# Merging and single-buffering four small tiles, so that the tiles behind them lie 128 bytes lower

## The chip, the cores and the metric

The kernel runs on one core of a Trainium2 chip. The metric is the device time of one execution in microseconds. The kernel before takes 742.22 us (median of three runs, 741.92 to 744.39).

## What is computed

Windowed attention with a linear bias, and a gated feed-forward layer on its output, all in float32:

```python
scores = scale * q @ k.T - slope[h] * dist       # 4 batches, 8 heads, 768 tokens, head size 64
scores = where(keep, scores, -1e9)               # first n_global keys, and the last n_local before a token
a = exp(scores - max); a = a / (sum(a) + 1e-9)
x = (a @ v) as [3072 tokens, 512]
out = (sigmoid(x @ w_gate) * (x @ w_val)) @ w_out   # inner size 1536
```

With the inputs that are timed, n_global is 8 and n_local is 96, so that a tile of 128 queries needs at most 256 keys.

## The kernel before

Tokens are worked off in eight blocks of 384 (`blocks`, half a batch each). While the feed-forward part of one block runs, the attention of the next block is woven into it. The feed-forward part of a block has twelve rounds, one for each 128 of the 1536 inner columns. In a round, `ff_in` does two groups of twelve matmuls (L564): the stationary operand is a 128x128 piece of `w1l` or `w1h` (gate and value weights, split into a high and a low part), the moving one 384 columns of `xh` or `xl` (the attention output, split in the same way). They end in the PSUM tiles `ps_g` and `ps_u`, from which ScalarE and VectorE make `work`, `hh` and `hl`. `ff_out` then does nine matmuls (L604): a 128x128 piece of `hh` or `hl` stands, 512 columns of `w2l` or `w2h` (output weights) move; only the first six rounds of the first block work with unsplit `hh` and `w2f`. Woven in between stand the score matmuls of a query tile (L387, four of 256 columns: `qs` stands, `ks` moves) and the matmuls with V (L502). The order on each engine is made when the kernel is built, by a list scheduler that works with a model of the instructions' times.

SBUF is given out by pools that lie one behind the other. Ahead of the pool `small` lie `wpool` (`w1h`, `w1l`, `w2f`), `cpool` and `xpool` (`xh`, `xl`). `small` holds tiles of a few bytes in each partition, and each of its buffers takes 32 bytes. Behind it lie `mpool` (`work`, `hl`, `hh`), `w2pool` (`w2h`, `w2l`), `rpool` (`kr`, the K columns), `spool` (`v0`, `v1`, `pT`), and behind those `wraw` (raw weights, while they are converted) and later `late` (`qr`, `qs`, `ks`, `halves`, `turned`, `pT2`, `ost`). What `small` takes therefore shifts everything behind it. In a `ks` tile, the key slots of successive query tiles lie 640 bytes apart, which is 128 more than 512.

At the end stands a general path, for values of n_local and n_global that the windowed scheme can't serve. Its test runs always: `top` is the largest of the row minima `nms` (L752), it is turned by TensorE (L754), reduced to one number (L756), and compared, with n_local and n_global, against bounds (L764); the five answers in `fl` give one flag (L766), and each engine branches on it. With the timed inputs the path itself (`dense_block`, with `gnm`, `gsm` and `grc`) is jumped over, and only a memset of `fl` (L844) runs in its place.

Of the kernel before, what the change touches and what calls it, by code (L numbers as in the profile page):

```python
# [8 lines left out]
F32 = mybir.dt.float32  # L9
# [10 lines left out]
P = 128  # L20
# [8 lines left out]
def attn_moe_kernel(ctx, tc, qT, kT, v, n_global, n_local, wg, wv, wo, out, B, H, S, D):  # L29
# [18 lines left out]
    small = ctx.enter_context(tc.tile_pool(name="small", bufs=4))  # L48
# [699 lines left out]
    general = ctx.enter_context(ExitStack())  # L748
    gpool = general.enter_context(tc.tile_pool(name="gpool", bufs=1))
    late["pool"] = gpool  # L750
    top = small.tile([P, 1], F32, name="top", bufs=1)
    nc.vector.tensor_reduce(top, nms, axis=AX.X, op=ALU.max)  # L752
    ps = ps_a.tile([P, 4, P], F32, name="ps_t")
    nc.tensor.transpose(ps[0:1, 0], top, ident)  # L754
    fl = small.tile([1, 5], F32, name="fl", bufs=1)
    nc.vector.tensor_reduce(fl[:, 4:5], ps[0:1, 0], axis=AX.X, op=ALU.max)  # L756
    for i, (src, bound, op) in enumerate((
        (nf[0:1, 0:1], 1.0, ALU.is_lt),
# [9 lines left out]
    def dense_tables(t):  # L768
        reli = gpool.tile([P, S], I32, name="reli")
        nc.gpsimd.iota(reli, pattern=[[-1, S]], base=t * P, channel_multiplier=1)  # L770
        rel = gpool.tile([P, S], F32, name="rel")
        nc.vector.tensor_copy(rel, reli)
        keep = gpool.tile([P, S], F32, name="keep")
        pen = gpool.tile([P, S], F32, name="pen")
        dist = gpool.tile([P, S], F32, name="dist")
        nc.vector.tensor_scalar(keep, rel, nf[:, 0:1], None, op0=ALU.is_lt)
        nc.vector.tensor_scalar(pen, rel, 0.0, None, op0=ALU.is_ge)
        nc.vector.tensor_tensor(keep, keep, pen, op=ALU.mult)
        nc.gpsimd.iota(reli, pattern=[[1, S]], base=0, channel_multiplier=0)
        glo = gpool.tile([P, S], F32, name="glo")  # L780
        nc.vector.tensor_copy(glo, reli)
        nc.vector.tensor_scalar(glo, glo, nf[:, 1:2], None, op0=ALU.is_lt)
        nc.vector.tensor_tensor(pen, glo, keep, op=ALU.mult)
        nc.vector.tensor_tensor(glo, glo, pen, op=ALU.subtract)

        nc.vector.tensor_tensor(dist, rel, keep, op=ALU.mult)
        nc.vector.tensor_scalar(pen, glo, nf[:, 0:1], None, op0=ALU.mult)
        nc.vector.tensor_tensor(dist, dist, pen, op=ALU.add)
        nc.vector.tensor_tensor(keep, keep, glo, op=ALU.add)
        nc.vector.tensor_scalar(pen, keep, 1.0, 1.0e9, op0=ALU.subtract, op1=ALU.mult)  # L790
        return keep, pen, dist

    def dense_block(b, t0, xh, xl):
        for t in range(TB):
            keep, pen, dist = dense_tables(t0 + t)
            for s in range(NPAIR):
                r0 = b * (H * D) + 2 * s * D
                qg = gpool.tile([P, P], F32, name="qg")
                nc.sync.dma_start(qg, qT[bass.ds(r0, P), (t0 + t) * P:(t0 + t + 1) * P])
                kg = gpool.tile([P, S], F32, name="kg")  # L800
                nc.sync.dma_start(kg, kT[bass.ds(r0, P), :])
                vg = gpool.tile([P, NTB, P], F32, name="vg")
                nc.sync.dma_start(
                    vg, v[bass.ds(b * S, S), s * P:(s + 1) * P].rearrange("(t p) x -> p t x", p=P)
                )
                nc.vector.tensor_scalar(qg, qg, SCALE, None, op0=ALU.mult)
                av = ps_a.tile([P, 4 * P], F32, name="ps_v")
                for j in range(2):
                    hd = slice(j * D, (j + 1) * D)
                    sb = gpool.tile([P, S], F32, name="sb")  # L810
                    for c in range(S // NB):
                        cols = slice(c * NB, (c + 1) * NB)
                        ps = ps_gv.tile([P, NB], F32, name=("ps_g", "ps_u")[c % 2])
                        nc.tensor.matmul(ps, qg[hd], kg[hd, cols], start=True, stop=True)
                        nc.vector.scalar_tensor_tensor(
                            sb[:, cols], dist[:, cols], -slopes[2 * s + j], ps, op0=ALU.mult, op1=ALU.add
                        )
                    nc.vector.tensor_tensor(sb, sb, keep, op=ALU.mult)
                    nc.vector.tensor_tensor(sb, sb, pen, op=ALU.add)
                    nm = small.tile([P, 1], F32, name="gnm", bufs=2)  # L820
                    nc.vector.tensor_reduce(nm, sb, axis=AX.X, op=ALU.max, negate=True)
                    sm = small.tile([P, 1], F32, name="gsm", bufs=2)
                    nc.scalar.activation(sb, sb, AF.Exp, bias=nm, accum_out=sm)
                    nc.vector.tensor_scalar(sm, sm, 1e-9, None, op0=ALU.add)
                    rc = small.tile([P, 1], F32, name="grc", bufs=2)
                    nc.vector.reciprocal(rc, sm)
                    nc.vector.tensor_scalar(sb, sb, rc, None, op0=ALU.mult)
                    pT = gpool.tile([P, NTB, P], F32, name="gpT")
                    for c0 in range(0, NTB, 3):
                        pt = ps_a.tile([P, 4, P], F32, name="ps_t")  # L830
                        for c in range(3):
                            nc.tensor.transpose(pt[:, c], sb[:, (c0 + c) * P:(c0 + c + 1) * P], ident)
                        nc.scalar.copy(pT[:, c0:c0 + 3], pt[:, 0:3])
                    for c in range(NTB):
                        nc.tensor.matmul(
                            av[hd, 0:P], vg[:, c, hd], pT[:, c], start=(c == 0), stop=(c == NTB - 1)
                        )
                cols = slice(t * P, (t + 1) * P)
                nc.scalar.activation(xh[:, s, cols], av[:, 0:P], AF.Copy)
                nc.vector.tensor_tensor(xl[:, s, cols], av[:, 0:P], xh[:, s, cols], op=ALU.subtract)  # L840
# [4 lines left out]
    with fits.Else():  # L845
        with tc.For_i(0, B, 1) as b:
            for t0 in range(0, NTB, TB):
                blocks.append((b, t0, TB))
                bi = len(blocks) - 1
                xslot[bi] = (0, NC * NB)  # L850
                dense_block(b, t0, *x_of(bi))
                for f in range(NF):
                    split_w2(f)
                    ff_in(bi, f)
                    ff_out(bi, f)
# [39 lines left out]
```

## Time and profile before

| | us |
|---|---|
| median of three runs | 742.22 |
| the profiled execution, its own time | 743.09 |
| its span, first to last instruction | 741.2 |
| TensorE busy with matmuls | 725.1 |
| VectorE busy | 499.8 |
| ScalarE busy | 420.3 |
| GpSimd busy | 218.8 |

The profiled execution lies 0.87 us above the median, and 1.9 us of its time lie outside its span. The end of a matmul is modelled in the trace, and a matmul begins before the one ahead of it has ended; so the pace of a row of matmuls is read from the distance between their starts, not from their durations.

### The profile page before, as it was taken

The numbers are of one execution on the slowest core, as the hardware profiler recorded it, in microseconds if no ns is written. First come the engines' busy times: TensorE is split into PE (matmuls) and PEld (weight loads), VectorE is DVE, ScalarE is ACT, GpSimd is POOL, SyncE is SP. The second block draws the span as 40 slices with busy tenths as digits, with TensorE's granted clock in tenths as the row PEclk, the third lists the DMA queues.
The fourth block names the chain that finished last, engine by engine and source line by source line (L and its number), as shares of the span: only waits on it lengthen the run. The fifth ranks groups of instructions, "written<-read, shape, count | busy, mean of one in ns | idle before, by whom it ended". The sixth has DMA issues, their size and how long they took to land. (4 is left out here: it accounts for less than half of the span.)

```text
span 741.2 us, 12477 instructions
## 1 busy us (share of the span) xinstructions
PE 725.1 (98%) x4403; PEld 657.2 (89%) x4403; DVE 499.8 (67%) x1303; ACT 420.3 (57%) x948; POOL 218.8 (30%) x166
## 2 busy tenths in 40 slices
PE   7999999999999999999999999999999999999997
PEld 6667778989889999999999999999999999999996
DVE  7889799667877777676677868666786876321111
ACT  5797887756565565566456655655555664332222
POOL 6424355323231323223132322313233231221222
PEclk9999999999999999999999999999999999999999
DMA  8967662624537343432435442343335224010001
GB/s 253 279 193 243 188 193 75 159 62 88 104 78 159 84 105 70 99 103 63 83 80 117 112 105 63 62 123 73 95 80 109 71 46 83 15 44 1 1 0 46
DMA packets 136866, 74.27 MB, mean 100 GB/s; under 512 B 87136, under 2 KB 129120, under 8 KB 136800
## 3 DMA queue, kind: packets, MB, share of 16 engines
q1 hardware_dynamic: 136800, 73.43, 40.1%
q8 instruction: 36, 0.59, 0.3%
q14 instruction: 30, 0.25, 0.1%
HBM read 49.81 MB, written 6.29 MB: 76 GB/s over the span
## 5 line engine op out<-in xcount | busy, mean ns | idle before, releaser
L180 POOL TENSOR_TENSOR w2l<-w2f,w2h 128x512 fp32r<-128x512 f32 x89 | 121.3, 1363 | 377.5 <-ACT w2h L217 363.7
L581 DVE SCALAR_TENSOR_TENSOR work<-work,ps_u 128x384 f32<-128x384 f32 x90 | 49.7, 552 | 131.0 <-PE ps_u L564 126.8
L564 PE MATMUL ps_g<-xh,w1l 128*128 128x384 f32 x384 | 131.9, 343 | 1.0 <-ACT work L572 1.0
L564 PE MATMUL ps_u<-xh,w1l 128*128 128x384 f32 x384 | 131.5, 342 | 0.1
L564 PE MATMUL ps_g<-xl,w1h 128*128 128x384 f32 x384 | 130.7, 340 | 0.7 <-DVE xl L545 0.7
L564 PE MATMUL ps_g<-xh,w1h 128*128 128x384 f32 x384 | 130.4, 340 | 0.0
L564 PE MATMUL ps_u<-xh,w1h 128*128 128x384 f32 x384 | 130.0, 339 | 0.0
L564 PE MATMUL ps_u<-xl,w1h 128*128 128x384 f32 x384 | 129.9, 338 | 0.0
L584 ACT ACTIVATE hh<-work 128x384 fp32r<-128x384 f32 x90 | 46.9, 522 | 132.4 <-DVE work L581 132.2
L419 ACT ACTIVATE work<-work,nms 128x256 f32<-128x256 f32 (+1 forms) x192 | 92.0, 480 | 27.5 <-DVE nms L406 27.1
L604 PE MATMUL ps_o<-w2l,hh 128*128 128x512 f32 x267 | 105.0, 393 | 0.4 <-POOL w2l L180 0.4
L604 PE MATMUL ps_o<-w2h,hh 128*128 128x512 f32 x267 | 105.1, 394 | 0.0
L604 PE MATMUL ps_o<-w2h,hl 128*128 128x512 f32 x267 | 104.5, 394 | 0.0
L180 DVE TENSOR_TENSOR hl<-work,hh 128x384 fp32r<-128x384 f32 x90 | 79.5, 884 | 23.5 <-ACT hh L584 23.3
L217 ACT ACTIVATE w2h<-w2f 128x512 fp32r<-128x512 f32 x89 | 56.0, 629 | 54.2 <-PE ps_o L604 52.6
L564 PEld LDWEIGHTS ps_g<-xh,w1l 128*128 128x128 f32 x384 | 72.7, 189 | 5.2 <-issue 2.8
L564 PEld LDWEIGHTS ps_u<-xh,w1l 128*128 128x128 f32 x384 | 72.2, 188 | 4.0 <-issue 1.2
L564 PEld LDWEIGHTS ps_g<-xl,w1h 128*128 128x128 f32 x384 | 72.7, 189 | 2.7 <-DVE xl L545 1.1
L564 PEld LDWEIGHTS ps_u<-xl,w1h 128*128 128x128 f32 x384 | 72.3, 188 | 1.1
L564 PEld LDWEIGHTS ps_g<-xh,w1h 128*128 128x128 f32 x384 | 72.7, 189 | 0.5 <-issue 0.2
L438 DVE TENSOR_SCALAR work<-work,rc 128x256 f32<-128x256 f32 (+1 forms) x168 | 71.6, 465 | 2.0
L564 PEld LDWEIGHTS ps_u<-xh,w1h 128*128 128x128 f32 x384 | 72.2, 188 | 0.0
(133 smaller groups left out, 1171.8 us busy)
## 6 DMA issues: line engine op xcount, KB each, us to landing
qr<-in_qT SPq DMA_DIRECT2D x56, 192.0 KB, 3.4
kr<-in_kT SPq DMA_DIRECT2D x32, 192.0 KB, 2.6
v<-in_v SPq DMA_DIRECT2D x32, 192.0 KB, 3.7
raw<-in_w_gate SPq DMA_DIRECT2D x12, 512.0 KB, 4.2
raw<-in_w_val SPq DMA_DIRECT2D x12, 512.0 KB, 5.6
raw<-in_w_out SPq DMA_DIRECT2D x12, 512.0 KB, 3.7
out<-ost SPq DMA_DIRECT2D x24, 256.0 KB, 2.2
v<-in_v SPq DMA_DIRECT2D x16, 144.0 KB, 3.8
```

The costliest lines, as they stand in the source:

```text
L180: eng.tensor_tensor(out, a, b, op=ALU.subtract)
L217: ins = nc.scalar.activation(hi, w, AF.Copy)
L419: ins = nc.scalar.activation(sb[:, j, :w], sb[:, j, :w], AF.Exp, scale=-1.0, bias=nm[:, j:j + 1], accum_out=sm[:, j:j + 1])
L438: nc.vector.tensor_scalar(sb[:, j, :w], sb[:, j, :w], rc[:, j:j + 1], None, op0=ALU.mult)
L564: nc.tensor.matmul(ps[:, :n], wt[f][:, i, c], xt[:, c, :n], start=(k == 0), stop=(k == 3 * NC - 1))
L581: nc.vector.scalar_tensor_tensor(a[:, :n], a[:, :n], 1.0, pss[1][:, :n], op0=ALU.add, op1=ALU.mult)
L584: nc.scalar.activation(hh[:, :n], a[:, :n], AF.Copy)
L604: ins = nc.tensor.matmul(outs[bi][t], ht[:, t * P:(t + 1) * P], wt, start=(f == 0 and k == 0), stop=(f == NF - 1 and k == len(parts) - 1),)
```

## The change

The test's two tiles become columns of one: `top` is column 0 of a 128x6 tile, `fl` the columns 1 to 5 of its first partition. In the general path, `gnm`, `gsm` and `grc` have one buffer instead of two. That makes four buffers of 32 bytes less in `small`, and everything that lies behind `small` moves down by 128 bytes in each partition. No instruction that runs with the timed inputs is added, removed or given another shape.

```diff
-    top = small.tile([P, 1], F32, name="top", bufs=1)
+    last = small.tile([P, 6], F32, name="top", bufs=1)
+    top = last[:, 0:1]
     nc.vector.tensor_reduce(top, nms, axis=AX.X, op=ALU.max)
     ps = ps_a.tile([P, 4, P], F32, name="ps_t")
     nc.tensor.transpose(ps[0:1, 0], top, ident)
-    fl = small.tile([1, 5], F32, name="fl", bufs=1)
+    fl = last[0:1, 1:6]
...
-                    nm = small.tile([P, 1], F32, name="gnm", bufs=2)
+                    nm = small.tile([P, 1], F32, name="gnm", bufs=1)
...
-                    sm = small.tile([P, 1], F32, name="gsm", bufs=2)
+                    sm = small.tile([P, 1], F32, name="gsm", bufs=1)
...
-                    rc = small.tile([P, 1], F32, name="grc", bufs=2)
+                    rc = small.tile([P, 1], F32, name="grc", bufs=1)
```

## Rows read from the trace of the kernel before

**Rows 1.** The page's head and its first part: busy time of each engine, share, instructions.
```profile
span 741.2 us, 12477 instructions
PE 725.1 (98%) x4403; PEld 657.2 (89%) x4403; DVE 499.8 (67%) x1303; ACT 420.3 (57%) x948; POOL 218.8 (30%) x166
```
**Rows 2.** Table of stretches, TensorE: stretch, length, busy (matmuls), clock, DMA share, GB/s.
```profile
0.00:45.00 45.00, 38.16 (x305) 1.00 0.79 232
486.80:572.60 85.80, 85.80 (x526) 1.00 0.39 90
660.00:741.20 81.20, 75.76 (x395) 0.99 0.06 20
```
**Rows 3.** Groups of instructions, TensorE, 231 to 660 us: count, busy us, mean ns.
```profile
L564 PE MATMUL ps_g<-xl,w1h 128*128 128x384 f32 x240 | 80.9, 337 | 0.0
...
L564 PE MATMUL ps_u<-xh,w1h 128*128 128x384 f32 x237 | 80.3, 339 | 0.0
...
L604 PE MATMUL ps_o<-w2h,hh 128*128 128x512 f32 x180 | 70.9, 394 | 0.0
```
**Rows 4.** The same groups in two short stretches, 722.85 to 724.94 and 721.95 to 722.85.
```profile
L564 PE MATMUL ps_u<-xh,w1h 128*128 128x384 f32 x4 | 1.3, 336 | 0.0
...
L604 PE MATMUL ps_o<-w2h,hh 128*128 128x512 f32 x2 | 0.8, 389 | 0.0
```
**Rows 5.** The same groups in two others, 716.55 to 718.66 and 714.47 to 716.55.
```profile
L564 PE MATMUL ps_u<-xh,w1h 128*128 128x384 f32 x4 | 1.4, 340 | 0.0
...
L604 PE MATMUL ps_o<-w2h,hh 128*128 128x512 f32 x3 | 1.2, 395 | 0.0
```
**Rows 6.** Timeline of TensorE, 716 to 730 us: start us, us, instruction.
```profile
716.56 0.34 PE L564 MATMUL ps_u<-xh,w1l 128*128 128x384 f32 x1
...
718.51 0.34 PE L564 MATMUL ps_u<-xh,w1h 128*128 128x384 f32 x1
...
722.86 0.34 PE L564 MATMUL ps_u<-xh,w1l 128*128 128x384 f32 x1
...
724.77 0.34 PE L564 MATMUL ps_u<-xh,w1h 128*128 128x384 f32 x1
...
727.03 0.39 PE L604 MATMUL ps_o<-w2l,hh 128*128 128x512 f32 x1
...
729.11 0.34 PE L564 MATMUL ps_u<-xh,w1l 128*128 128x384 f32 x1
```
**Rows 7.** Table of stretches, all engines (PE, PEld, DVE, ACT, POOL busy), same stretch.
```profile
716.50:729.10 12.60, 12.60 (x67) 11.81 (x67) 2.23 (x4) 3.81 (x7) 3.37 (x3) 1.00 0.00 1
```
**Rows 8.** Timeline of TensorE, 318 to 326 us.
```profile
318.19 0.64 PE L387 MATMUL ps_s<-ks,qs 128*128 128x256 f32 x4
318.67 0.39 PE L604 MATMUL ps_o<-w2l,hh 128*128 128x512 f32 x1
...
320.70 0.34 PE L564 MATMUL ps_g<-xh,w1l 128*128 128x384 f32 x1
...
324.87 0.64 PE L387 MATMUL ps_s<-ks,qs 128*128 128x256 f32 x4
325.34 0.34 PE L564 MATMUL ps_g<-xh,w1l 128*128 128x384 f32 x1
```
**Rows 9.** Timeline of VectorE, 6 to 7 us and 658 to 659 us.
```profile
6.21 0.32 DVE L764 TENSOR_SCALAR fl<-nf 1x1 f32<-1x1 f32 x4
...
658.21 0.28 DVE L756 TENSOR_REDUCE fl<-ps_t 1x1 f32<-1x128 f32 x1 [0.42 <-PE ps_t L754]
```
**Rows 10.** Table of stretches, TensorE, around 60 us.
```profile
58.00:59.00 1.00, 0.00 (x0) 1.00 0.73 234
...
61.00:62.00 1.00, 1.00 (x5) 0.50 1.01 396
```
**Rows 11.** Timeline of TensorE, 60 to 64 us.
```profile
60.90 0.52 PE L564 MATMUL ps_g<-xh,w1l 128*128 128x384 f32 x1
...
63.46 0.47 PE L564 MATMUL ps_g<-xh,w1h 128*128 128x384 f32 x1
```

## The prediction

> **What bounds the kernel now.** I began with the busy times of the page: TensorE is busy with matmuls for 725.1 of 741.2 us, and no other engine for more than 499.8 [rows 1]. The table of stretches says where the remaining 16 us are: 6.8 in the first 45 us, where K, Q and the raw weights arrive, and 5.4 behind 660 us; in the stretch of a whole block there is no gap at all, 85.80 of 85.80 us [rows 2]. So in between, the time is the number of matmuls times their pace, and a change that adds and removes no instruction can only act through that pace, through the two ends, or through the order of the instructions.
>
> Therefore I read the pace next, from the starts of the matmuls in the timeline. It has two levels with the same operands. From 716.56 to 718.51 lie eleven distances between L564 matmuls, 1.95 us or 177 ns each; from 722.86 to 724.77 eleven more, 1.91 us or 174 ns each [rows 6]. For L604 the nine distances from 727.03 to 729.11 make 231 ns each [rows 6], and the nine from 318.67 to 320.70 make 226 ns [rows 8]. A round of 24 matmuls at L564 and nine at L604 is thus 0.09 + 0.05 us dearer at the slow pace (24 x 3.6 ns and 9 x 5.5 ns). The granted clock is 1.00, 2.4 GHz, through the stretch in which the pace switches [rows 7]. The mean durations follow the pace: 336 and 389 ns in fast stretches [rows 4], 340 and 395 in slow ones [rows 5]. Over 231 to 660 us the groups have 337 to 339 and 394 [rows 3]. For L604 that is (394 - 389) / (395 - 389), or 0.8 of the rounds at the slow pace. For L564 it is between 0.25 and 0.75, and rather too much, since a matmul behind a pause counts long too; I take 0.45.
>
> What sets the pace? Not other engines: in the stretch of rows 6, where it switches, VectorE is busy for 2.23, ScalarE for 3.81 and GpSimd for 3.37 of 12.6 us [rows 7], and the pace holds over whole groups. It is what went before. A round of L604 that follows directly on fast L564 matmuls is slow (727.03), and one that follows on a score group is fast (318.67) [rows 6, 8].
>
> The Trainium skill says in SBUF — State Buffer, section "Who interferes with whom", that TensorE and ScalarE never wait for another engine's access to SBUF. By that alone the place of a tile would be worth nothing and the time 742.2 us; by the rows the pace moves by 2 to 3% without another engine's help, which the rule neither foresees nor forbids, and the sum would lie anywhere between the bounds below. The trace agrees with the rule in that the switch doesn't follow the other engines.
>
> **The change, part by part.**
>
> The general path (three tiles with one buffer instead of two) doesn't run: what it would wait for costs 0. Its code may become some instructions longer or shorter, and the branch jumps over it. That lies behind the last L604 matmul; I take 0.
>
> The test: top and fl share a tile. The danger is order. Four of the five comparisons, L764, need only n_local and n_global, and the scheduler has put them at 6.21 us, 652 us ahead of L756 at 658.21, which in the program comes before them and writes the same tile fl, another column [rows 9]. So a tile's columns are followed one by one, and columns 1 to 4 of the shared tile can be written as early as before. Cost 0. If I am wrong, four instructions of together 0.32 us leave VectorE's queue in the first stretch and stand behind L756 at 658 us, where TensorE is far ahead in work. At most 0.3 us would be gained at the start, and nothing lost at 658 us. I count 0, and bound it by -0.3 and 0.
>
> The shift by 128 bytes. It touches the operands of L604 (hh, hl, w2h, w2l), L387 (ks, qs) and L502 (V, pT), and what VectorE, ScalarE, GpSimd and the DMAs read and write. It doesn't touch those of L564, for w1 and x lie ahead of the pool small. The trace has no move by 128 bytes of the same operand, but one near it: the key slots of successive score groups lie 128 bytes more than 512 apart. Four score matmuls take 318.67 - 318.19 = 0.48 us in one and 325.34 - 324.87 = 0.47 us in the next [rows 8], so a step of 128 bytes is worth at most 10 ns in 480, 2%, and the two groups are followed by different matmuls, which may be all of it. On the nine matmuls of L604 in 90 rounds (96 less the six unsplit ones) 2% would be 90 x 9 x 4.6 ns = 3.7 us either way; the direct cost I take is 0, because both operands of every shifted matmul move by the same amount and keep their distance.
>
> What remains is the hand-over, where a matmul with unshifted operands (L564) follows on one with shifted ones, or the reverse. If it depends on addresses, rounds change their pace. All of L604 and L564 fast would be 90 x 0.8 x 0.05 = 3.6 us and 96 x 0.45 x 0.09 = 3.9 us less, 7.5 in all; all slow 90 x 0.2 x 0.05 = 0.9 and 96 x 0.55 x 0.09 = 4.8 us more, 5.7 in all. Between -7.5 and +5.7 I take 0, by the row that is nearest, the two score groups, which differ by no more than the last digit.
>
> The first 45 us: transfers into shifted tiles. TensorE lacks 6.8 us there for all reasons together [rows 2], and nothing in the rows speaks for a transfer that is longer or shorter by its address; I take 0 and allow 0.5 either way.
>
> A shift of some tenths in the start can also move the half clock. After a time without a matmul at 58 to 59 us, TensorE is granted 0.50 of its clock, 1.2 instead of 2.4 GHz, at 61 to 62 us [rows 10], and from 60.90 to 63.46 eight matmuls come 320 ns apart [rows 11] instead of 174: 1.2 us that can go, or come a second time at another gap.
>
> Sum: 743.09 + 0 = 743.09 us against the profiled execution, which lay 0.87 above the median; so 742.2 us for a median.
>
> **The rivals.**
>
> *The fast hand-over.* The slow rounds of L604 are those behind fast L564 matmuls, the commonest sequence. If with the lower addresses this hand-over behaves as that behind a score group, L604 runs at 226 ns and the next L564 group starts fast. For it: most of L604 is on the slow side today (0.8), so there is more to win than to lose there. Against it: no row shows that an address decides it, and the time since the last pause could as well. Half of the 7.5 us gives 738.5 us. It passes 0.3% (2.2 us) when three rounds in ten turn.
>
> *The slow hand-over.* Slower than before: L564 is fast today in about half of its groups, those that follow on scores, V matmuls or a fast L604. If the last shifted operand ahead of them now leaves them at the slow pace, each round pays 0.09 us. Two thirds of the 4.8 us gives 745.4 us; it passes 0.3% when half of the fast groups turn. For it: L564 is the larger part of the matmuls. Against it: it needs the good hand-overs to go bad, all at different addresses.
>
> *The half clock goes or comes twice*: 741.0 or 743.4 us, within the forecast.
>
> *The comparisons move*: 741.9 us, within the forecast. That the change does nothing at all to the pace is the forecast itself.
>
> **How the numbers follow.** A measurement of this kernel tells about 0.3%, 2.2 us, from no change. No change that can be measured: 0.44, with a range of its own from 740.0 to 744.4. The fast hand-over: 0.33. The slow one: 0.23. The trace shows that the pace hangs on small things, which keeps the two rivals together above the forecast; it shows no address that decides it, which keeps each of them below it. The range of 8 in 10 reaches into both: down to 737.6, a little below the fast rival's time, and up to 745.8, a little above the slow one's.
>
> **What would show each step right or wrong.** Right: L604 with w2h and hh at a mean of 394 and L564 at 337 to 339 ns in the stretch from 231 to 660 us, a block of 85.8 us, L764 four times near 6.2 us. Fast hand-over: a mean of L604 near 389 to 391, with 226 ns between starts directly behind L564. Slow hand-over: L564 groups at 340 to 341. If the mean durations stay and the time moves, the step on the pace is wrong and the cause lies in the first 60 us, in the clock or in the order of instructions; if the number of matmuls between the stages differs, the step on the scheduler is wrong.

## The result and the profile after

The kernel after takes 736.58 us (median of seven runs, 735.94 to 741.15), the kernel before 743.28 in the runs made beside it (741.92 to 745.74). The ratio is 0.992, with a 95% interval from 0.989 to 0.995. That is faster by more than the 0.3% of the prediction, and 1.0 us under the low end of its range. The profiled execution took 736.18 us.

The page's head and its first part, of the kernel after, beside [rows 1]:

```profile
span 734.4 us, 12477 instructions
...
PE 718.1 (98%) x4403; PEld 653.0 (89%) x4403; DVE 498.8 (68%) x1303; ACT 420.2 (57%) x948; POOL 219.4 (30%) x166
```

Every engine ran as many instructions as before. The span fell by 6.8 us and TensorE's busy time by 7.0, while VectorE, ScalarE and GpSimd moved by 1.0 us at most. TensorE does the same matmuls in less time.

Table of stretches, TensorE, of after (stretch, length, busy and matmuls, granted clock, DMA share, GB/s). The second is the stretch around [rows 10, 11], the third holds the same 526 matmuls as the block of [rows 2], and the fourth the same 395 as its last stretch:

```profile
0.00:45.00 45.00, 37.57 (x303) 1.00 0.77 229
58.00:66.00 8.00, 7.27 (x54) 1.00 0.91 301
482.07:567.47 85.40, 85.40 (x526) 1.00 0.40 91
653.78:734.40 80.62, 75.05 (x395) 0.99 0.06 21
```

A block has no gap, as before, and takes 85.40 us instead of 85.80. The stretch from 58 to 66 us in the kernel before:

```profile
58.00:66.00 8.00, 6.61 (x44) 0.79 0.88 278
```

Groups of instructions on TensorE from 231 to 660 us in after, the lines of [rows 3] (count, busy us, mean ns):

```profile
L564 PE MATMUL ps_g<-xl,w1h 128*128 128x384 f32 x244 | 82.1, 336 | 0.0
...
L564 PE MATMUL ps_u<-xh,w1h 128*128 128x384 f32 x240 | 80.7, 336 | 0.0
L604 PE MATMUL ps_o<-w2h,hh 128*128 128x512 f32 x181 | 70.6, 390 | 0.0
```

L604 went from 394 to 390 ns and L564 from 337 and 339 to 336, which are, within 1 ns, the means of the fast stretches of [rows 4]. The timeline of TensorE in after shows a round of L604 directly behind L564 (start us, us, instruction):

```profile
707.60 0.34 PE L564 MATMUL ps_g<-xh,w1h 128*128 128x384 f32 x1
707.77 0.39 PE L604 MATMUL ps_o<-w2l,hh 128*128 128x512 f32 x1
...
709.81 0.34 PE L564 MATMUL ps_u<-xh,w1l 128*128 128x384 f32 x1
```

The nine distances from 707.77 to 709.81 make 227 ns each. In the kernel before, the same nine matmuls lie from 714.48 to 716.56, 231 ns each: the matmul at 709.81 is the one at 716.56 of [rows 6], and that at 707.77 is this one of before:

```profile
714.48 0.39 PE L604 MATMUL ps_o<-w2l,hh 128*128 128x512 f32 x1
```

**Where the 6.8 us came from.** Both kernels run the same 4403 matmuls in the same order, so the same matmul can be followed through both timelines. The one at 60.90 of [rows 11] starts at 59.99 in after, 0.9 us earlier; the one at 63.46 starts at 61.38, 2.1 earlier; the one at 716.56 starts at 709.81, 6.75 earlier. So 0.9 us came before 61 us, 1.2 from the half clock of [rows 10, 11], which this execution of after didn't have, and 4.7 from the pace of the matmuls in the 650 us behind it. The timelines of TensorE around 59 us show the first two, first before and then after (in brackets the idle time ahead and what ended it):

```profile
59.39 0.48 PE L373 MATMUL ps_v<-kr,qr 64*128 64x256 f32 x1 [1.84 <-DVE nms L406]
...
60.58 0.52 PE L564 MATMUL ps_g<-xh,w1h 128*128 128x384 f32 x1
60.90 0.52 PE L564 MATMUL ps_g<-xh,w1l 128*128 128x384 f32 x1
```

```profile
58.73 0.48 PE L373 MATMUL ps_v<-kr,qr 64*128 64x256 f32 x1 [0.84 <-DVE nms L406]
...
59.82 0.34 PE L564 MATMUL ps_g<-xh,w1h 128*128 128x384 f32 x1
59.99 0.34 PE L564 MATMUL ps_g<-xh,w1l 128*128 128x384 f32 x1
```

TensorE waited 1.84 us for VectorE's `nms` in the one and 0.84 in the other. Behind the long wait the matmuls come 320 ns apart, behind the short one 170. Neither is shown to come from the change. The wait differs from execution to execution: all_up128 below has the pace of before and a wait of 0.46 us. And a long wait doesn't always bring the half clock: TensorE waited 1.78 us in gnm_only, 1.85 in w2_up64 and 1.90 in kv_back, and was granted 1.00 from 58 to 66 us in all three. Here is gnm_only (wait, then stretch):

```profile
60.13 0.48 PE L373 MATMUL ps_v<-kr,qr 64*128 64x256 f32 x1 [1.78 <-DVE nms L406]
```

```profile
58.00:66.00 8.00, 6.22 (x51) 1.00 0.85 279
```

The 4.7 can be read from the starts in the timelines. From 100 us in the kernel before to the matmul at 716.56, the distances between the same matmuls add up to 4.5 us less in after: 2.2 us between two matmuls of L604, 1.8 between two of L564, and 0.5 in all other places. It can also be counted in groups. Behind 100 us I called an L564 group of twelve slow when its mean distance, the first distance left out, is above 175 ns, and an L604 round slow when it is above 230.3 ns. A slow L564 group costs 12 x 3.4 = 41 ns (176.8 instead of 173.4 ns a matmul), a slow round of L604 9 x 4.9 = 44 ns (231.6 instead of 226.7). A "decaying" round begins slow and becomes fast within its nine matmuls; where the line is drawn moves the counts of L604 by a few rounds.

```
                            before   after
L564 groups, slow / fast    70/105   6/169
L604 rounds, slow / decaying / fast   64/17/8   4/12/72
L604 directly behind fast L564        53 slow of 54   58 fast of 60
L564 directly behind L604             32 slow of 51   0 slow of 51
```

64 groups x 41 ns and 60 rounds x 44 ns are 2.6 + 2.6 = 5.2 us, an estimate that is 0.7 above the 4.5 read directly.

**What the median holds besides.** A half clock like that of [rows 10] comes in some executions and not in others, of either kernel. The 110 executions of the kernel before, in all comparisons below, have a median of 741.6 us where the mean granted clock of the execution was 0.998 or more (44 of them) and of 744.8 where it was 0.993 or less. The four executions of after at 0.998 have 736.2. At like clock the change is worth 5.4 us (0.7%), near the 4.7 of pace in the profiled pair and the 5.0 that up128 shows below. The remaining 1.3 of the 6.7 us between the medians I put down to how many half-clock stretches fell into these seven and seven runs; the granted clock of all seven runs of before is not on record, so this isn't shown.

### The profile page after: what moved, and what is told of

It reads as the page before. It is cut to its first block, busy times and chain, and to the rows that moved or that the text cites. A ratio compares the mean times of both kernels' runs of the same rounds, so it can differ in the third digit from the quotient of the medians.

```text
span 734.4 us, 12477 instructions
## 1 busy us (share of the span) xinstructions
PE 718.1 (98%) x4403; PEld 653.0 (89%) x4403; DVE 498.8 (68%) x1303; ACT 420.2 (57%) x948; POOL 219.4 (30%) x166
## 5 line engine op out<-in xcount | busy, mean ns | idle before, releaser
L564 PE MATMUL ps_g<-xh,w1l 128*128 128x384 f32 x384 | 131.1, 341 | 1.0 <-ACT work L572 1.0
L564 PE MATMUL ps_u<-xh,w1l 128*128 128x384 f32 x384 | 130.9, 341 | 0.1
L564 PE MATMUL ps_g<-xl,w1h 128*128 128x384 f32 x384 | 129.6, 337 | 0.7 <-DVE xl L545 0.7
L564 PE MATMUL ps_g<-xh,w1h 128*128 128x384 f32 x384 | 129.4, 337 | 0.0
L564 PE MATMUL ps_u<-xh,w1h 128*128 128x384 f32 x384 | 129.3, 337 | 0.0
L564 PE MATMUL ps_u<-xl,w1h 128*128 128x384 f32 x384 | 129.2, 336 | 0.0
L604 PE MATMUL ps_o<-w2l,hh 128*128 128x512 f32 x267 | 104.9, 393 | 0.6 <-POOL w2l L180 0.5
L604 PE MATMUL ps_o<-w2h,hh 128*128 128x512 f32 x267 | 104.1, 390 | 0.0
L604 PE MATMUL ps_o<-w2h,hl 128*128 128x512 f32 x267 | 103.1, 389 | 0.0
L564 PEld LDWEIGHTS ps_g<-xh,w1l 128*128 128x128 f32 x384 | 72.2, 188 | 5.1 <-issue 2.3
L564 PEld LDWEIGHTS ps_u<-xh,w1l 128*128 128x128 f32 x384 | 72.1, 188 | 3.9 <-issue 1.2
L564 PEld LDWEIGHTS ps_g<-xl,w1h 128*128 128x128 f32 x384 | 72.2, 188 | 2.6 <-DVE xl L545 1.1
L564 PEld LDWEIGHTS ps_u<-xl,w1h 128*128 128x128 f32 x384 | 72.2, 188 | 1.0
L564 PEld LDWEIGHTS ps_g<-xh,w1h 128*128 128x128 f32 x384 | 72.2, 188 | 0.5 <-issue 0.2
L564 PEld LDWEIGHTS ps_u<-xh,w1h 128*128 128x128 f32 x384 | 72.2, 188 | 0.0
```

The source lines that it names most:

```text
L564: nc.tensor.matmul(ps[:, :n], wt[f][:, i, c], xt[:, c, :n], start=(k == 0), stop=(k == 3 * NC - 1))
L604: ins = nc.tensor.matmul(outs[bi][t], ht[:, t * P:(t + 1) * P], wt, start=(f == 0 and k == 0), stop=(f == NF - 1 and k == len(parts) - 1),)
```

## The experiments

**The theory:** TensorE's pace hangs on where the operands of one stage lie against those of the other (w1 and x of L564 on one side, hh, hl and w2 of L604, K and V on the other). **The rivals:** the absolute address, so that lower is faster; the merged tile or the single buffers themselves, by order or by waits; and the distance of the two operands within a stage.

The last two columns are the counts from the timeline of each profiled execution; "at 0.998" is the median of the executions at that mean granted clock or more, with their number.

```
kernel       behind small lies   median us  ratio [95%]            at 0.998    L564 slow  L604 slow/decaying
before       as it is            743.3      1                      741.6 (44)  70         64/17
after        -128                736.58     0.992 [0.989, 0.995]   736.2 (4)    6          4/12
up128        +128                737.35     0.991 [0.989, 0.993]   736.5 (2)    6          3/14
up256        +256                742.97     1.000 [0.998, 1.002]   741.5 (4)   67         63/18
all_up128    +128, w1, x too     742.90     0.999 [0.997, 1.002]   740.9 (4)   70         63/16
low64        -64                 741.42     0.996 [0.995, 0.998]   739.6 (3)    5         66/4
up64         +64                 744.48     1.002 [1.000, 1.003]   none       115         12/73
merge_only   -32                 738.11     0.994 [0.992, 0.997]   737.5 (3)   10          6/11
gnm_only     -32                 739.20     0.996 [0.994, 0.999]   738.0 (4)   12          8/8
single_buf   -96                 742.34     0.999 [0.998, 1.000]   740.5 (4)   85         27/51
merge_96     -96                 742.08     0.999 [0.997, 1.001]   741.5 (5)   88         25/51
```

### Absolute place or distance

all_up128 moves everything, w1 and x too, by 128 bytes, so that only the distance to SBUF's start changes:

```diff
-    w1h = [wpool.tile([P, 2, NC, P], F32R, name=f"w1h{f}") for f in range(NF)]
+    first = wpool.tile([P, 2 * NC * P + 32], F32R, name="w1h0")
+    w1h = [first[:, 32:].rearrange("p (i c n) -> p i c n", i=2, c=NC)]
+    w1h += [wpool.tile([P, 2, NC, P], F32R, name=f"w1h{f}") for f in range(1, NF)]
```

> Everything from the weights on, the unshifted operands of L564 too, lies 128 bytes higher than before; hh, hl, w2h and w2l keep their distance to w1 and x. Theory A, the distance between the operand that goes and the one that comes at a hand-over decides the pace: as before, 743 us, L604 w2h,hh at a mean of 394 ns from 231 to 660 us. Theory B, the place of an operand itself decides it, in steps that repeat each 256 bytes: as after, 736.6 us and 390 ns. Theory C, the place itself, with any other repeat: open, but L564 can change its pace too, now that w1 and x have moved.

Measured: 742.90 us, ratio 0.999 (0.997 to 1.002). The groups of TensorE, 231 to 660 us (its L566 and L606 are L564 and L604):

```profile
L566 PE MATMUL ps_u<-xh,w1h 128*128 128x384 f32 x238 | 80.6, 339 | 0.0
...
L606 PE MATMUL ps_o<-w2h,hh 128*128 128x512 f32 x180 | 70.9, 394 | 0.0
```

The means are those of before, and so are the counts. Matmul for matmul, the distances within L564 and within L604 add up to the same as before to 0.03 us. What counts is the place of tiles against each other; a move of all operands in SBUF by 128 bytes does nothing.

### Which tiles

hh_low is the kernel after with w2 and all behind it back at their places of before, so that only work, hh and hl are 128 bytes lower:

```diff
-            hi = w2pool.tile([P, DM], F32R, name="w2h")
+            hi = w2pool.tile([P, DM + 32], F32R, name="w2h")[:, 32:]
```

> work, hl and hh lie 128 bytes lower as in the changed kernel; w2h, w2l, K, V and all behind them lie where they lay before. Theory S, the standing operand decides at the hand-over from L564 to L604 (hh is loaded while xh moves): as after, 736 to 738 us, L604 w2h,hh at 390 ns. Theory M, the moving operand decides (w2h moves while w1 is loaded): as before, 742 to 744 us, 394 ns. Theory R, within L604 the distance of standing and moving operand decides, which is 128 bytes less here than in both kernels: neither, L604 different from both.

Measured: 741.79 us, 0.998 (0.996 to 1.000). w2_up is the same edit on the kernel before: hh and hl stay, w2 and all behind it lie 128 bytes higher.

> work, hl and hh lie where they lay before; w2h, w2l, K, V and all behind them lie 128 bytes higher than before. Theory M, the moving operand decides, with a repeat of 256 bytes: as after, 736 to 738 us, L604 w2h,hh at 390 ns. Theory S, the standing operand decides: as before, 742 to 744 us and 394 ns. Theory R, the distance of the two within L604: neither of the two, as in the kernel with hh alone low.

Measured: 743.22 us, 1.000 (0.998 to 1.002). The groups of hh_low and then of w2_up, 231 to 660 us:

```profile
L564 PE MATMUL ps_u<-xh,w1h 128*128 128x384 f32 x237 | 79.9, 337 | 0.0
...
L604 PE MATMUL ps_o<-w2h,hh 128*128 128x512 f32 x180 | 70.9, 394 | 0.0
```

```profile
L564 PE MATMUL ps_u<-xh,w1h 128*128 128x384 f32 x240 | 80.7, 336 | 0.0
...
L604 PE MATMUL ps_o<-w2l,hh 128*128 128x512 f32 x180 | 71.3, 396 | 0.0
```

In both, the distance of hh and w2 differs from that of before by 128 bytes, and in both all 89 rounds of L604 are slow, also the 24 behind a score group, of which only about a third are slow in the kernel before. Neither the theory of the standing operand nor that of the moving one foresaw this; the third, the distance within L604, had named a pace different from both kernels. So the distance within a stage counts too, and the gain of the change needs hh and w2 to move together. In w2_up nearly all of L564 is fast (one slow group of 176) though every round of L604 ahead of it is slow: the two stages' paces aren't one state that is handed on.

kv_back is the kernel after with K, V, pT, qs and ks back at their places, so that only work, hh, hl and w2 are lower:

```diff
-            lo = w2pool.tile([P, DM], F32R, name="w2l")
+            lo = w2pool.tile([P, DM + 32], F32R, name="w2l")[:, :DM]
```

> work, hl, hh, w2h and w2l lie 128 bytes lower as in the changed kernel; K, V, pT, qs, ks and all behind them lie where they lay before. If the gain is made at L604 and its hand-overs alone: as after, 736.6 us within 1 us, L604 w2h,hh at 390 ns. If the scores and the V matmuls carry part of it: between 737.5 and 742 us, with L604 still at 390 but L564 ps_u<-xh,w1h above 336 ns.

Measured: 737.95 us, 0.994 (0.992 to 0.997); 737.8 at a granted clock of 0.998 or more, against 736.2 of after. L604 directly behind fast L564 is fast, as in after (49 of 50). What is lost stands mostly behind scores: 14 of the 50 L564 groups behind a score group are slow (1 in after), 7 of the 24 rounds of L604 there (1 in after), and so are the 11 rounds of L604 behind slow groups of L564. In all 23 L564 groups and 19 rounds of L604 are slow, against 6 and 4: (17 x 41) + (15 x 44) ns = 1.4 us, near the 1.5 measured. So K, V, pT, qs and ks carry about a quarter of the gain, by the same switch between the two paces.

### How the pace goes with the distance

up128 is the kernel before with a longer `flag` tile: all behind `small` lies 128 bytes higher instead of lower, nothing is merged and all buffers stay two. up256 has 256 bytes.

```diff
-    flag = small.tile([1, 1], I32, name="flag", bufs=1)
+    flag = small.tile([1, 33], I32, name="flag", bufs=1)[:, 0:1]
```

> The flag's tile is 128 bytes longer, and everything behind the small tiles lies 128 bytes higher than before, with n_local, w1 and x in place. The all-up run has shown that only the distance to w1 and x counts. Theory P256, that distance counts in steps that repeat each 256 bytes: +128 is then the same as -128, so as after, 736.6 us, with L604 w2h,hh at 390 ns and L564 ps_u<-xh,w1h at 336. Theory P512 or longer: another time, most likely as before, 743 us, with 394 and 339 ns, since nothing singles out this distance.

Measured: 737.35 us, 0.991 (0.989 to 0.993).

> Everything behind the small tiles lies 256 bytes higher than before. Theory P256: as before, 743 us, 394 and 339 ns. Theory P512 or longer: open, 735 to 745 us, and the pace different from both.

Measured: 742.97 us, 1.000 (0.998 to 1.002). The groups of up128 and then of up256, 231 to 660 us:

```profile
L564 PE MATMUL ps_u<-xh,w1h 128*128 128x384 f32 x240 | 80.7, 336 | 0.0
...
L604 PE MATMUL ps_o<-w2h,hh 128*128 128x512 f32 x183 | 71.3, 390 | 0.0
```

```profile
L564 PE MATMUL ps_u<-xh,w1h 128*128 128x384 f32 x236 | 79.9, 339 | 0.0
...
L604 PE MATMUL ps_o<-w2h,hh 128*128 128x512 f32 x180 | 70.9, 394 | 0.0
```

128 higher is 128 lower, to within two rounds of the counts, and 256 higher is no shift at all. The pattern repeats every 256 bytes, and the change gains by nothing but its 128 bytes: up128 has neither the merge nor the single buffers. Its stretch from 58 to 66 us is at half clock like that of before, so its profile shows the pace alone:

```profile
58.00:66.00 8.00, 6.28 (x42) 0.79 0.90 269
```

Its matmul at 63.61 is the one at 63.46 of [rows 11], 0.15 us later, and the one at 711.75 that at 716.56 of [rows 6], 4.8 earlier: 5.0 us of pace.

w2_up384 is w2_up with 384 instead of 128 bytes, a test of the same period within the stage:

```diff
-            hi = w2pool.tile([P, DM], F32R, name="w2h")
+            hi = w2pool.tile([P, DM + 96], F32R, name="w2h")[:, 96:]
```

> work, hl and hh lie as before, w2h, w2l and all behind them 384 bytes higher. Theory P256: the same as with w2 128 bytes higher, 743.2 us, all rounds of L604 slow (395 ns) and L564 fast (336 ns). Theory P512: 384 up is 128 down, the distance of hh to w2 has the other sign than in the two runs in which L604 was slow throughout; L604 can then be faster than there, below 393 ns, and the time below 741 us.

Measured: 740.90 us, 0.997 (0.995 to 1.000), with 2 slow groups of L564 and all 88 rounds of L604 slow, the pattern of w2_up (1 and 89). The time alone would have fitted the theory of 512 bytes, which had named less than 741 us; but its sign, L604 below 393 ns, didn't come. The medians differ by 2.3 us, and so do the clocks: all five executions of w2_up384 were at 0.998 or more, and one of ten of w2_up, which took 741.6.

low64 is the kernel after with 17 instead of 1 in `flag`, so that the shift is 64 bytes down; up64 is the kernel before with 17, 64 bytes up.

> Everything behind the small tiles lies 64 bytes lower than before, half of the change. Theory steps (two places, good and bad, that alternate each 128 bytes): as before, 743 us, or as after, 736.6 us. Theory slope (a collision that gets longer the nearer two addresses are): between, 738 to 742 us.

Measured: 741.42 us, 0.996 (0.995 to 0.998): L564 as fast as in after, L604 as slow as in before (59 of the 61 rounds directly behind fast L564). The time lies in the range named for a slope, but not by one: each stage is wholly at one of the two paces.

> Everything behind the small tiles lies 64 bytes higher than before, the last quarter of the 256. Theory H has no number for this distance; half way between a place with slow L604 and slow L564 (before) and one with both fast (128 higher): L604 and L564 each either slow or fast, 737 to 743 us. A slope would give 740 us with both in between.

Measured: 744.48 us, 1.002 (1.000 to 1.003), the slowest of all: 115 slow groups of L564, and 73 rounds of L604 that decay. That lies outside everything that was expected. The groups of low64 and then of up64:

```profile
L564 PE MATMUL ps_u<-xh,w1h 128*128 128x384 f32 x240 | 80.7, 336 | 0.0
...
L604 PE MATMUL ps_o<-w2h,hh 128*128 128x512 f32 x180 | 70.9, 394 | 0.0
```

```profile
L564 PE MATMUL ps_g<-xh,w1h 128*128 128x384 f32 x238 | 80.6, 339 | 0.0
...
L604 PE MATMUL ps_o<-w2h,hh 128*128 128x512 f32 x180 | 70.5, 392 | 0.0
```

### One operand of L564 alone

These were to show which distance sets the pace of which stage. x_alone moves xh and xl 128 bytes up and all behind them 256, so that only x changes its distances; w1_alone moves w1 and w2f 128 up and the rest by 0 or 256.

```diff
-    xall = [xpool.tile([P, 2 * NC * NB], F32R, name=name) for name in ("xh", "xl")]
+    xall = [xpool.tile([P, 2 * NC * NB + n], F32R, name=name)[:, n:] for name, n in (("xh", 32), ("xl", 0))]
```

> xh and xl alone lie 128 bytes higher; what lies behind the small tiles lies 256 higher, which the runs so far show to be worth nothing. So hh stands to xh (the hand-over from L564 to L604) as in the changed kernel, w2h stands to w1 (the hand-over back) as before, and within L564 w1 stands to x in a new way. Theory H, each hand-over sets the pace of the stage behind it: L604 fast, w2h,hh at 390 ns, and L564 in part slow, 337 to 340 ns; 738 to 741 us. Theory N, the distance within a stage sets its pace: L604 as before, 394 ns, and L564 anything, 735 to 750 us.

Measured: 742.75 us, 1.000 (0.997 to 1.002). L604 directly behind fast L564 decays in 26 rounds and is slow in 10, where before it was slow in 53 of 54; but 115 groups of L564 are slow. Neither theory had this.

> w1 alone (with w2f) lies 128 bytes higher, all else at the place of before or 256 above it. hh stands to xh as before, w2h to w1 as in the changed kernel, w1 to x as in the run with x alone. Theory H: L604 slow, 394 ns, L564 fast, 336 ns; 739 to 742 us. Theory N: L604 as before, 394 ns, and L564 the same as in the run with x alone, whatever that is.

Measured: 739.46 us, 0.995 (0.994 to 0.997). 32 groups of L564 are slow, less than half of before; L604 directly behind fast L564 decays in 22 rounds, is slow in 13 and fast in one. The time lies in the range of theory H, but L604 isn't slow throughout, as that theory had it.

w2_up64 is w2_up with 64 bytes:

```diff
-            hi = w2pool.tile([P, DM], F32R, name="w2h")
+            hi = w2pool.tile([P, DM + 16], F32R, name="w2h")[:, 16:]
```

> w2h, w2l and all behind them lie 64 bytes higher, work, hl and hh as before. Theory N for L604, any distance other than 0 between hh and w2 makes it slow: all rounds slow, 394 ns or more. Theory H alone: hh stands to xh as before, so L604 as before, 394 ns with some rounds fast behind scores. L564: w2h stands to w1 as in no run yet, between the place of before and that of 128 higher.

Measured: 742.21 us, 0.998 (0.996 to 1.000). L604 is slow in 37 rounds and decays in 51, fast in none, where theory N had expected all rounds slow.

Neither operand alone brings what both together bring: moving x or w1 alone turned "slow" into "decaying", and none made the hand-over fast as the shift of both distances does. That one pair of operands alone sets the pace of a stage, which I had taken from the first experiments, fell here.

### The two parts of the change, each alone

merge_only has the merge of `top` and `fl` alone, and so everything 32 bytes lower; single_buf has the three single buffers alone, 96 bytes lower.

```diff
-    top = small.tile([P, 1], F32, name="top", bufs=1)
+    last = small.tile([P, 6], F32, name="top", bufs=1)
+    top = last[:, 0:1]
...
-    fl = small.tile([1, 5], F32, name="fl", bufs=1)
+    fl = last[0:1, 1:6]
```

> One part of the change alone: the test's two tiles merged, gnm, gsm and grc with two buffers as before; everything behind the small tiles lies 32 bytes lower. Placement (only the distances between the operands of L604 and those of L564 count, repeating each 256 bytes): the pace lies between that of no shift (L604 394, L564 339 ns) and that of 64 bytes lower (394, 336), so 741.4 to 743.3 us. The merge itself as the cause: about 736.6 us with L604 at 390 ns.

Measured: 738.11 us, 0.994 (0.992 to 0.997).

> The other part alone: gnm, gsm and grc with one buffer, the test's tiles apart as before; everything behind the small tiles lies 96 bytes lower. Placement: the pace lies between that of 64 bytes lower (L604 394, L564 336 ns) and that of 128 lower (390, 336), so 736.6 to 741.4 us, with part of the L604 rounds behind fast L564 groups fast. Sum of the parts (if the merge were the cause): as before, 743.3 us with L604 at 394 and L564 at 339.

Measured: 742.34 us, 0.999 (0.998 to 1.000). Both lie outside what I had expected of placement, which took the pace to go by degrees from 0 to 128 bytes: 32 bytes brought 4.1 us at like clock and 96 next to nothing, as if the merge had done it. So the corners that were missing were run: gnm_only is 32 bytes lower without the merge (one buffer for `gnm` alone), and merge_96 is the whole change with a `flag` tile longer by 32 bytes, 96 lower with the merge.

```diff
-                    nm = small.tile([P, 1], F32, name="gnm", bufs=2)
+                    nm = small.tile([P, 1], F32, name="gnm", bufs=1)
```

> 32 bytes lower without the merge: only gnm has one buffer instead of two, top and fl stay apart. If 32 bytes of placement make the gain seen with the merge alone: about 738.1 us, L604 at 391 and L564 at 336 to 339 ns, no slow L604 behind fast L564. If the merge itself makes it (by order or by what the tile's sharing changes): about 743 us, L604 at 394.

Measured: 739.20 us, 0.996 (0.994 to 0.999).

```diff
-    flag = small.tile([1, 1], I32, name="flag", bufs=1)
+    flag = small.tile([1, 9], I32, name="flag", bufs=1)[:, 0:1]
```

> The whole change with the flag's tile 24 bytes wider by one buffer step, so that everything behind the small tiles lies 96 instead of 128 bytes lower, with the merge. If placement decides: as with the single buffers alone, about 742 us, half of the L564 groups slow and L604 behind fast L564 decaying from slow to fast, 392 ns. If the merge makes the gain: about 737 us.

Measured: 742.08 us, 0.999 (0.997 to 1.001). The groups of merge_only, gnm_only, single_buf and merge_96, in this order, 231 to 660 us:

```profile
L564 PE MATMUL ps_u<-xh,w1h 128*128 128x384 f32 x240 | 80.6, 336 | 0.0
L604 PE MATMUL ps_o<-w2h,hh 128*128 128x512 f32 x181 | 70.7, 391 | 0.0
```

```profile
L564 PE MATMUL ps_u<-xh,w1h 128*128 128x384 f32 x240 | 80.8, 337 | 0.0
...
L604 PE MATMUL ps_o<-w2h,hh 128*128 128x512 f32 x182 | 71.2, 391 | 0.0
```

```profile
L564 PE MATMUL ps_u<-xh,w1h 128*128 128x384 f32 x239 | 80.8, 338 | 0.0
...
L604 PE MATMUL ps_o<-w2h,hh 128*128 128x512 f32 x180 | 70.5, 392 | 0.0
```

```profile
L564 PE MATMUL ps_u<-xh,w1h 128*128 128x384 f32 x240 | 81.2, 338 | 0.0
...
L604 PE MATMUL ps_o<-w2h,hh 128*128 128x512 f32 x180 | 70.5, 392 | 0.0
```

The pairs agree by the bytes, whether the tiles are merged or not: at -32, 10 and 12 slow groups of L564 and 6 and 8 slow rounds of L604; at -96, 85 and 88, and 27 and 25. The merge does nothing; 32 bytes bring most of what 128 bring, and 64 and 96 in between don't. The pace does not go by degrees with the distance, and no run here gives a rule by which a good distance could be worked out.

## Why the prediction was wrong

**What bounds the kernel, and that only the pace can move:** right. The counts of instructions are the same, the block has its 526 matmuls in both, and no gap [rows 1, 2]. The two ends hold 12.2 of the 16.1 us in which TensorE is idle; the prediction left out the rest, of which 1.4 lie from 58 to 66 us.

**That the pace has two levels with the same operands, and follows what went before and not the other engines:** right, and what the pace gained is rounds that changed their level. In two stretches of the kernel before, the other engines do nearly the same and the pace differs: from 716.56 to 718.51 VectorE is idle, ScalarE is busy for 0.63 us and GpSimd for 0.98, and from 722.86 to 724.77 0, 0.63 and 0.94; no DMA moves data in either, and twelve L564 matmuls start 177 ns apart in the first and 174 in the second. So the other engines' tiles, which moved too, aren't needed to explain the two levels. The sizes of the prediction were a little high. All-fast was worked out as 3.6 us of L604 and 3.9 of L564; by the counts the slow ones of before were 64 of 89 rounds (0.8 taken, with 17 more that decay) and 70 of 175 groups (0.45 taken), and by the estimate above (44 and 41 ns) they were worth 2.8 and 2.9 us, 5.7 in all.

**The hand-over, taken as 0 "by the row that is nearest, the two score groups":** this is the step that failed. It turned to fast in 58 of 60 rounds behind L564, and in all 51 L564 groups behind L604, and with the groups that follow on these it brought the 4.5 us read above (5.4 at like clock) instead of 0. The row could not carry it. The distance of 0.48 and 0.47 us is taken inside a group of four matmuls of one stage, of which only `ks` steps by 128 bytes, and it says nothing of the first matmuls behind a change of stage. The nearer rows were those on which the prediction had just seen the pace switch, [rows 6, 8]: L604 slow behind L564 and fast behind a score group. They had the same operands, and only the operands ahead were others. That makes the place of those against each other a cause to be reckoned with, with no row against it; 0 was a choice between unknown bounds, not a reading.

**The direct cost of the shift, taken as 0 because both operands keep their distance:** consistent with the runs, and the condition behind it, that both operands move together, was more important than the prediction says. When hh and w2 do not move together, all rounds of L604 are slow (hh_low, w2_up, w2_up384).

**The fast hand-over, a rival at 738.5 us:** this is what happened, with the signs that the prediction named for it (L604 at 389 to 391 ns, 226 ns between starts directly behind L564; measured 389 to 391, and 227). Its size was set to half of 7.5 us. Nearly all of what there was to win was won, 5.2 us of the 5.7 by the same estimate. For want of a row on the share that turns, half was a guess.

**The half clock, 1.2 us as a rival within the forecast:** its size was right (2.56 us for eight distances from 60.90 to 63.46 before, 1.39 after), but I kept it as a case of its own, where it comes on top of any of the others. The profiled executions lie 6.9 us apart: 4.7 of pace, 1.2 of half clock, 0.9 ahead of 61 us, and less than 0.2 behind the last round compared. The range ended at 737.6 because it took the fast hand-over at half and without the half clock. That the median lies below it owes something to the clock: 743.28 less the 5.4 us at like clock would be 737.9, just inside. The forecast of no change was wrong by those 5.4 us all the same.

**The comparisons of the test:** right. In after they stand early, four times, 0.13 us each (duration ns min/median/max, first and last start):

```profile
L765 DVE TENSOR_SCALAR top<-nf x4: 131/131/135, 6.2 to 6.4; 1x1 f32<-1x1 f32 x4
```

**The general path and the start, taken as 0:** the matmul that started at 45.05 starts at 45.41 in after, 0.4 us later, within the 0.5 allowed; and from the matmul at 735.39 (728.51 in after) to the end of the span 5.8 and 5.9 us pass.

The prediction weighed the rule of the Trainium skill, SBUF — State Buffer, section "Who interferes with whom", that TensorE never waits for another engine's access to SBUF. The traces agree with it as far as they go: with the other engines' work nearly the same in the two stretches above (0.63 us of ScalarE and 0.98 or 0.94 of GpSimd), the pace was 177 and 174 ns. What fell is the reading that a tile's place is then worth nothing. By that reading up128 would have stayed at 743.3 us; it took 737.35.

**What stays open** is what in TensorE makes the difference. The runs show that it hangs on the operands' distances within 256 bytes, across stages and within one, and that no single pair decides it. The tiles K, V, pT, qs and ks were moved only together. Whether it lies in the loading of the stationary operand, in the reading of the moving one, or in both, no run here tells apart.

## What to carry to other kernels

When TensorE is the bound without gaps, and the same matmul has two paces in the trace with what ran ahead of it as the only difference, take the place of the operands as a live cause: pad one small tile by 32, 64, 96 and 128 bytes and time each, and read the pace by distances between starts, not by the total alone, which here moved by 3 us with the granted clock. An edit that changes only dead tiles isn't free of effect, since it moves all tiles behind it; compare it with a kernel that is padded to the same addresses before its gain is put down to what it does. Where an unknown has wide bounds and no row in favour of 0, give the ends their chances, and let effects that are independent of each other add up in the range.

## What the runs showed of the hardware

- A shift of 128 bytes up or down of hh, hl, w2, K and V against w1 and x is worth 5.1 to 5.4 us of 741.6 at like clock; 256 bytes are worth nothing that the runs tell. A matmul of 512 columns takes 226.7 or 231.6 ns from start to start, one of 384 columns 173.4 or 176.8, at a granted clock of 1.00, 2.4 GHz.
- The pace lasts over a group and often into the next, but a round can also begin slow and become fast within its nine matmuls; in the kernel 64 bytes up 73 of 89 rounds of L604 do so.
- The half clock (1.2 GHz) can also come early in an execution. In the profiled execution of single_buf the stretch from 8 to 24 us was granted 0.68 on the mean, with 82 matmuls, in that of after 1.00, with 121:

```profile
8.00:24.00 16.00, 14.36 (x82) 0.68 0.87 275
```

```profile
8.00:24.00 16.00, 12.79 (x121) 1.00 1.03 329
```

  Executions of one and the same kernel differ by this: 110 of the kernel before lay between 740.0 and 746.6 us, with 3.2 us between the medians of those at a mean granted clock of 0.993 or less and of 0.998 or more. Near 60 us the clock fell behind a wait of 1.84 us in the profiled executions of before and up128, and not behind waits of 1.78 to 1.90 in gnm_only, w2_up64 and kv_back. So the length of the wait alone doesn't decide it; what does, and what makes the waits differ between executions, the runs don't show.
